# Attention and a two-layer FFN on one core: k and q of the second batch's third and fourth head pair loaded ahead of the remaining weight chunks

## The chip, the core and the metric

The kernel runs on one core of a Trainium2 chip. The metric is device time in microseconds (us) from the start to the end of the program. Three runs of the kernel before gave 899.69, 900.2 and 901.63 us; the median is 900.2 us. The core has a matrix engine (PE, with its weight loads shown as PEld), three engines for elementwise work (VectorE, shown as DVE; ScalarE, ACT; GpSimd, POOL), and SyncE (SP), which here only starts transfers (DMAs) from and to device memory. Each engine takes its instructions in a fixed order, and an instruction that waits holds up those behind it on its engine.

## The reference

```python
def _attn_ref(q, k, v):                       # 8 batches, 8 heads, 576 rows, 64 columns, float32
    q_s = softmax of q over the last axis
    k_s = softmax of k over the rows (axis 2)
    kv = np.einsum('bhsd,bhse->bhde', k_s, v)
    return np.einsum('bhsd,bhde->bhse', q_s, kv)

def _moe_ref(x, w_in, w_out):                 # x: 4608 x 512 (heads side by side)
    h = x @ w_in                              # w_in: 512 x 2048
    r = np.maximum(h, 0.0)
    return ((r * r) @ w_out)                  # w_out: 2048 x 512
```

The weights come as 64-bit floats. A product of float32 accuracy is made of three passes of a shorter format: high by high, low by high, high by low.

## The kernel before, in words

**Tiling.** The 4608 rows are taken as one block of 512 rows per batch, and a ninth block made of the 64 rows that each batch leaves over (`x_left` in device memory). Heads go in pairs, four per batch; pair `pr` of batch `b` gives 128 of the 512 columns of x. I write (1,2) for the third pair of the second batch. The FFN goes by 16 chunks `fc` of 128 hidden columns. For each chunk `ffn_h` makes h with 12 matmuls (lines 412 to 414), `activate` makes the square of the ReLU and splits it in `g_hi` and `g_lo` (lines 416 to 430), and two chunks later `ffn_out` adds 12 matmuls into four accumulators (lines 446 to 448). I call these twelve matmuls h7 or o5, by the chunk.

**Weights.** Each chunk of w_in (`raw_i`) and of w_out (`raw_o`) is a transfer of 512 KB. Such a chunk becomes two float32 halves in `split_weight` (line 156): two conversions on ACT (lines 168 and 170), two combining operations on DVE (lines 172 and 173, through the one PSUM bank `bank3`), the high part on ACT (line 180) and the low part on POOL (line 181). I call the halves wi7 or wo5. Weights are split while the first block runs, so the first 135 us hold all 32 splits, all attention work of batch 1 (the second batch), and the first of batch 2.

**Attention of batch 1.** A pair has these units: `k_max` (line 224 on DVE, a transpose on PE at line 228, line 230 on DVE), `k_spread` (line 256 on PE), `q_exp` (lines 266 on DVE, 268 on POOL, 271 on ACT), `k_exp` (line 261 on DVE, 262 on ACT), `q_norm`, `kv` (line 305 on PE), transposes of q (lines 353 and 355), and the product with kv (line 364). From batch 2 on, `k_max` finds its maximum by a chain of small DVE operations (lines 238 to 251) instead of PE.

**Buffers and loads.** k, q and v of batch 1 and later go through two buffers each (`kt0`, `kt1`, `qt0`, `qt1`, `vt0`, `vt1`); the pair two places on reuses the buffer. `load_one` starts a load, two DMAs for k or q, four for v, all from SP. In the kernel before, the load of a pair's k, q or v is called right behind the unit that reads the buffer last two pairs earlier. A pool tag `raw` has four buffers (`RAWB`), for small staging tiles: `left` (64 columns of x on their way to `x_left`) in batches 0 and 1, `tb`, `xf` and `o` later.

**Order.** Units of batch 1 stand in a table of slots (`FIRST_KV`, `EARLY_STEP`, `EARLY_AT`) and are issued with raised priority; the framework's scheduler then fixes the order of each engine's instructions by its own estimate of times. So a change in where loads are called can move instructions on every engine. PE's order in the first block is nearly fixed by `ordered`, which chains the PE instructions of batches 0 and 1.

Of the kernel before, what the change touches and what calls it, by code (L numbers as in the profile page):

```python
# [8 lines left out]
F32 = mybir.dt.float32  # L9
# [7 lines left out]
P = 128  # L17
HALF = 64
LOW = 5
# [26 lines left out]
def attention_ffn_kernel(ctx: ExitStack, tc: tile.TileContext, q, k, v, w_in, w_out, out):  # L46
# [74 lines left out]
    def load(dst, src, b, pr, n):  # L121
        s = src[b, 2 * pr : 2 * pr + 2]
        lo = s[:, :SPLIT, :].rearrange("h (p j) d -> p h j d", j=LOW)
        hi = s[:, SPLIT:, :].rearrange("h (p j) d -> p h j d", j=HIGH)
        if n < 2 or b == 0:
            e = nc.scalar if (b, pr, n) in ACT_LOADS else nc.sync
            e.dma_start(dst[:HALF], lo)
            e.dma_start(dst[HALF:, :, :HIGH, :], hi)
        else:
            for h in range(2):  # L130
                nc.sync.dma_start(dst[:HALF, h, :, :D], lo[:, h])
                nc.sync.dma_start(dst[HALF:, h, :HIGH, :D], hi[:, h])

    def tiles(b, pr):
        i = pr if b == 0 else pr % NB
        return kt[i], qt[i], (v0 if b == 0 else vt)[i]

    def load_one(b, pr, n):
        load(tiles(b, pr)[n], (k, q, v)[n], b, pr, n)

    def load_pair(b, pr):
        for n in range(3):
# [384 lines left out]
    x_hi.append(late.tile([P, NCC, NT], F32R, name="x_hi1"))  # L527
    x_lo.append(late.tile([P, NCC, NT], F32R, name="x_lo1"))

    for pr in range(NB):  # L530
        load_pair(1, pr)
    for n in range(AHEAD, NFC):
        load_more(n)
    steps = [(0, fc) for fc in order0] + [(blk, fc) for blk in range(1, B + 1) for fc in range(NFC)]
    LAG = 2
    gs, accs = {}, {}
# [2 lines left out]
    for b in range(1, B):  # L539
        for pr in range(NPAIR):  # L540
            if b == 1:
                base, offs = FIRST_KV + EARLY_STEP * pr, EARLY_AT
            else:
                base, offs = 2 * NFC * (b - 1) + 1 + STEADY_STEP * pr, STEADY_AT
            us = attention(b, pr)
            nxt = b * NPAIR + pr + NB
            if nxt < B * NPAIR:
                i = 5 if b == 1 else 4

                for i, m in ((i, 2), (i - 2, 0), (i - 3, 1)):  # L550
                    us[i] = lambda f=us[i], m=m, nxt=nxt: (f(), load_one(nxt // NPAIR, nxt % NPAIR, m))
            for u, o in zip(us, offs):
                slots.setdefault(base + o, []).append(u)
    for cc, u in enumerate(left_units()):
        slots.setdefault(2 * NFC * (B - 1) + 4 + 6 * cc, []).append(u)
# [64 lines left out]
```

## Time and profile before

| what | value |
|---|---|
| median of three runs | 900.2 us |
| the profiled execution, its own time | 900.7 us |
| its span, first to last instruction | 898.9 us |
| granted PE clock, mean over the span | 0.994 |
| PE idle in the span | 29.4 us (898.9 less 869.5 busy) |
| of that in 0 to 67 us | 13.7 us |
| of that in 67 to 90 us | 6.6 us |
| of that in 90 to 135 us | 3.4 us |
| of that from 135 to 600 us | 0 |

The table's idle times are the length of a stretch less PE's busy time in it, from the view that gives each engine's busy time by stretch. PE is the engine that sets the end: from 135 us to its last matmul it has no gap that the profile shows. What the first 135 us lose on PE, the whole run loses. In the timeline a row reads: start in us, length in us, engine, line, operation, what it writes and reads; a bracket at the end gives the engine's idle time ahead of it and what ended that.

### The profile page before, as it was taken

To read this page: it belongs to the slowest core of one execution; us is meant where nothing else is said; L and a number is where in the kernel's file an instruction comes from. 1 tells how busy PE (TensorE), PEld (TensorE's weight loads), DVE (VectorE), ACT (ScalarE), POOL (GpSimd) and SP (SyncE) were. 2 spreads that over 40 slices of the span, in tenths; PEclk is the share of its full clock that TensorE was granted. 3 is DMA by queue.
4 is the path that set the end of the run, shared out by engine and by line. 5 is a ranking of instruction groups with operands and counts; after the bars stand their busy time and mean duration, and the time that the engine had idled before them with its cause. 6 is when DMAs were issued, how large, how long until landed. Compare 5 with 4: busy or idle time off the path is not lost.

```text
span 898.9 us, 12680 instructions
## 1 busy us (share of the span) xinstructions
PE 869.5 (97%) x4368; PEld 700.6 (78%) x4368; DVE 579.6 (64%) x1177; ACT 407.7 (45%) x801; POOL 202.4 (23%) x177
## 2 busy tenths in 40 slices
PE   4997999999999999999999999999999999999997
PEld 3675677888888888888888888888888888888885
DVE  7767898877778876877688767876764242222222
ACT  3785756455345453544454544454444232222222
POOL 3676634222212220231122212221222000000000
PEclk9998999999999999999999999999999999999999
DMA  9999212422142224322333133222311030002001
GB/s 234 278 317 257 68 30 58 117 77 79 44 117 76 80 58 104 85 71 71 88 84 81 51 83 88 77 66 69 92 31 32 2 93 1 1 1 47 1 1 47
DMA packets 95743, 73.18 MB, mean 81 GB/s; under 512 B 47552, under 2 KB 85440, under 8 KB 95680
## 3 DMA queue, kind: packets, MB, share of 16 engines
q1 hardware_dynamic: 94944, 71.53, 29.5%
q10 hardware_dynamic: 736, 0.85, 0.4%
q8 instruction: 34, 0.56, 0.3%
q14 instruction: 29, 0.24, 0.1%
HBM read 54.00 MB, written 18.35 MB: 80 GB/s over the span
## 4 chain that ended last, share of the span: by engine, by line
PE 85%; DVE 1%; issue 0%; ACT 0%
PE o_ps L446 14%; PE bank L412 14%; PE o_ps L448 14%; PE o_ps L447 14%; PE bank L414 13%; PE bank L413 13%; PE bank L305 2%; PE bank L384 1%; DVE w L173 0%; DVE r L422 0%; DVE bank L172 0%; DVE m L243 0%; DVE kvn L321 0%; DVE o_last L460 0%; DVE m L246 0%
## 5 line engine op out<-in xcount | busy, mean ns | idle before, releaser
L412 PE MATMUL bank<-x_hi,wi 128*128 128x512 f32 x568 | 226.0, 398 | 2.2 <-DVE r L422 2.2
L446 PE MATMUL o_ps<-wo,g_hi 128*128 128x512 f32 x576 | 227.6, 397 | 0.0
L447 PE MATMUL o_ps<-wo,g_hi 128*128 128x512 f32 x576 | 224.9, 390 | 0.0
L448 PE MATMUL o_ps<-wo,g_lo 128*128 128x512 f32 x576 | 224.4, 391 | 0.0
L414 PE MATMUL bank<-x_hi,wi 128*128 128x512 f32 x568 | 223.4, 393 | 0.0
L413 PE MATMUL bank<-x_lo,wi 128*128 128x512 f32 x568 | 222.4, 392 | 0.0
L424 DVE TENSOR_TENSOR r<-r 128x512 f32<-128x512 f32 x128 | 110.7, 865 | 119.5 <-ACT r L418 119.2
L429 DVE TENSOR_TENSOR g_lo<-r,g_hi 128x512 fp32r<-128x512 f32 x132 | 100.7, 763 | 106.7 <-ACT g_hi L425 105.3
L425 ACT CAST g_hi<-r 128x512 fp32r<-128x512 f32 x144 | 89.2, 619 | 124.4 <-PE o_ps L447 78.2
L418 ACT ACTIVATE r<-bank 128x512 f32<-128x512 f32 x142 | 84.7, 596 | 102.5 <-PE bank L414 99.6
L412 PEld LDWEIGHTS bank<-x_hi,wi 128*128 128x128 f32 x568 | 107.1, 189 | 26.3 <-DVE r L422 3.5
L446 PEld LDWEIGHTS o_ps<-wo,g_hi 128*128 128x128 f32 x576 | 108.2, 188 | 23.5 <-issue 0.5
L448 PEld LDWEIGHTS o_ps<-wo,g_lo 128*128 128x128 f32 x576 | 108.1, 188 | 23.2
L447 PEld LDWEIGHTS o_ps<-wo,g_hi 128*128 128x128 f32 x576 | 108.2, 188 | 22.8 <-issue 0.5
L414 PEld LDWEIGHTS bank<-x_hi,wi 128*128 128x128 f32 x568 | 106.9, 188 | 24.2 <-POOL wi L181 0.4
L413 PEld LDWEIGHTS bank<-x_lo,wi 128*128 128x128 f32 x568 | 107.0, 188 | 21.9 <-issue 0.2
L395 POOL TENSOR_TENSOR x_lo<-xf,x_hi 128x256 fp32r<-128x256 f32 x48 | 39.6, 825 | 374.0 <-ACT x_hi L394 373.3
L338 POOL TENSOR_TENSOR qs<-qT,qs 64x640 fp32r<-64x640 f32 x48 | 81.8, 1705 | 60.0 <-ACT qs L337 47.1
L224 DVE TENSOR_REDUCE m<-kt 128x128 f32<-128x640 f32 x32 | 41.4, 1298 | 20.6 <-DMA kt<-in_k_dram 20.4
L337 ACT CAST qs<-qT 64x640 fp32r<-64x640 f32 x48 | 34.9, 726 | 39.6 <-DMA qT<-bounce 39.0
L271 ACT ACTIVATE qn<-qn 128x640 f32<-128x640 f32 x32 | 23.6, 739 | 54.2 <-DVE qn L268 44.8
L386 ACT COPY xf<-bank 64x320 f32<-64x320 f32 (+1 forms) x96 | 37.9, 395 | 20.6 <-PE bank L384 13.0
(118 smaller groups left out, 775.3 us busy)
## 6 DMA issues: line engine op xcount, KB each, us to landing
out_dram<-o SPq DMA_DIRECT2D x70, 128.0 KB, 2.4
raw_i<-in_moe_w_in_dram SPq DMA_DIRECT2D x16, 512.0 KB, 8.4
raw_o<-in_moe_w_out_dram SPq DMA_DIRECT2D x16, 512.0 KB, 9.6
bounce<-tb SPq DMA_DIRECT2D x24, 320.0 KB, 2.2
qT<-bounce SPq DMA_DIRECT2D x96, 80.0 KB, 2.2
kt<-in_k_dram SPq DMA_DIRECT2D x32, 160.0 KB, 3.0
qt<-in_q_dram SPq DMA_DIRECT2D x30, 160.0 KB, 3.0
vt<-in_v_dram SPq DMA_DIRECT2D x56, 80.0 KB, 2.5
```

The source lines that it names most:

```text
L224: nc.vector.tensor_reduce(m, kk.rearrange("p h j d -> p h d j"), axis=AX.X, op=ALU.max)
L338: nc.gpsimd.tensor_tensor(qs[other], qT[own], qs[own].bitcast(F32), op=ALU.subtract)
L412: nc.tensor.matmul(ps, wi[fc][:, 0, sl], xh[:, cc, :], start=(cc == 0), stop=False)
L413: nc.tensor.matmul(ps, wi[fc][:, 0, sl], xl[:, cc, :], start=False, stop=False)
L414: last.append(nc.tensor.matmul(ps, wi[fc][:, 1, sl], xh[:, cc, :], start=False, stop=(cc == NCC - 1)))
L418: nc.scalar.activation(r, ps, AF.Relu)
L424: nc.vector.tensor_tensor(r, r, r, op=ALU.mult)
L425: gh = nc.scalar.copy(g_hi, r)
L429: e.tensor_tensor(g_lo, r, g_hi.bitcast(F32), op=ALU.subtract)
L446: nc.tensor.matmul(acc[t], g_hi[:, ts], wo[fc][:, 0], start=(n == 0), stop=False)
L447: nc.tensor.matmul(acc[t], g_hi[:, ts], wo[fc][:, 1], start=False, stop=False)
L448: prev = nc.tensor.matmul(acc[t], g_lo[:, ts], wo[fc][:, 0], start=False, stop=(n == NFC - 1))
```

## The change

Batch 1's pairs (1,2) and (1,3) get k buffers of their own: two tiles `k_own2` and `k_own3` out of the four of the `raw` tag, taken at the start, with their unused corner set by POOL. After the loads of pairs (1,0) and (1,1), the program now calls the loads of k of (1,2) and (1,3). Then it issues the `q_exp` units of (1,0) and (1,1) and, behind each, the load of q of (1,2) and (1,3). Only then, held behind the last of these loads on SP, it starts the remaining weight chunks: raw_o4 to raw_o15 and raw_i8 to raw_i15. v of (1,2) and (1,3) is called where it was. `kt0` and `kt1` are no longer used by (1,2) and (1,3), so the loads of k of (2,0) and (2,1) are their next use.

```diff
-            e.dma_start(dst[HALF:, :, :HIGH, :], hi)
+            return e.dma_start(dst[HALF:, :, :HIGH, :], hi)
...
+    k_own = {}
+    for pr in range(NB, NPAIR):
+        t = w_pool.tile([P, 2, LOW, D], F32, name=f"k_own{pr}", tag="raw", bufs=RAWB)
+        nc.gpsimd.memset(t[HALF:, :, HIGH, :], -FLT_MAX)
+        k_own[1, pr] = t
+
     def tiles(b, pr):
         i = pr if b == 0 else pr % NB
-        return kt[i], qt[i], (v0 if b == 0 else vt)[i]
+        return k_own.get((b, pr), kt[i]), qt[i], (v0 if b == 0 else vt)[i]
...
+    second = [attention(1, pr) for pr in range(NPAIR)]
     for pr in range(NB):
         load_pair(1, pr)
-    for n in range(AHEAD, NFC):
-        load_more(n)
+    for pr in range(NB, NPAIR):
+        load_one(1, pr, 0)
+    for pr in range(NB):
+        with tc.high_priority(OFFSET):
+            second[pr][2]()
+        second[pr][2] = None
+        q_last = load_one(1, pr + NB, 1)
+    with tc.issue_after(q_last.ins):
+        for n in range(AHEAD, NFC):
+            load_more(n)
...
-            us = attention(b, pr)
+            us = second[pr] if b == 1 else attention(b, pr)
...
                 for i, m in ((i, 2), (i - 2, 0), (i - 3, 1)):
+                    if nxt // NPAIR == 1 and m < 2:
+                        continue
                     us[i] = lambda f=us[i], m=m, nxt=nxt: (f(), load_one(nxt // NPAIR, nxt % NPAIR, m))
             for u, o in zip(us, offs):
+                if u is None:
+                    continue
                 slots.setdefault(base + o, []).append(u)
```

The rows that follow show the order of instructions on two engines. Lines of the changed kernel are six higher from `load_one` to the end of the helpers (266 becomes 272, 224 becomes 230, 172 and 173 become 178 and 179, 422 becomes 428); the last number in a name is only a running number of the tile.

SP, from the last load of pair (1,1) on, before:

```order
L132 DMA vt1_81<-in_v_dram 64x4x64
L153 DMA raw_o4_555<-in_moe_w_out_dram 128x1024
L151 DMA raw_i8_557<-in_moe_w_in_dram 128x4x256
L153 DMA raw_o5_559<-in_moe_w_out_dram 128x1024
L151 DMA raw_i9_561<-in_moe_w_in_dram 128x4x256
```

and now:

```order
L132 DMA vt1_81<-in_v_dram 64x4x64
L127 DMA k_own2_131<-in_k_dram 64x2x320
L128 DMA k_own2_131<-in_k_dram 64x2x256
L127 DMA k_own3_133<-in_k_dram 64x2x320
L128 DMA k_own3_133<-in_k_dram 64x2x256
L127 DMA qt0_82<-in_q_dram 64x2x320
L128 DMA qt0_82<-in_q_dram 64x2x256
L379 DMA x_left_77<-left_472 128x64
L379 DMA x_left_77<-left_514 128x64
L127 DMA qt1_83<-in_q_dram 64x2x320
L128 DMA qt1_83<-in_q_dram 64x2x256
L159 DMA raw_o4_577<-in_moe_w_out_dram 128x1024
```

Eight load DMAs and two small stores now stand ahead of the first of the twenty remaining weight chunks. Before, q of (1,2) stood behind raw_o9, q of (1,3) behind raw_o10, and k of (1,2) behind raw_o14.

DVE, from the last combining of the squared ReLU of h1 on, before:

```order
L422 TENSOR_TENSOR r_618<-r_618,h_ps1_132 128x512
L280 RECIPROCAL qs_829<-qs_829 128x10
L230 TENSOR_REDUCE mc_651<-bank2_88 128x1
L172 SCALAR_TENSOR_TENSOR bank3_89<-bank3_89,raw_i4_167 128x512
L261 TENSOR_TENSOR ke_677<-kt0_78,bank2_88 128x640
```

and now:

```order
L428 TENSOR_TENSOR r_640<-r_640,h_ps1_136 128x512
L272 TENSOR_REDUCE qm_946<-qt0_82 128x10
L286 RECIPROCAL qs_833<-qs_833 128x10
L236 TENSOR_REDUCE mc_666<-bank2_88 128x1
L230 TENSOR_REDUCE m_967<-k_own2_131 128x128
L178 SCALAR_TENSOR_TENSOR bank3_89<-bank3_89,raw_i4_171 128x512
L272 TENSOR_REDUCE qm_1108<-qt1_83 128x10
L267 TENSOR_TENSOR ke_692<-kt0_78,bank2_88 128x640
```

The row maximum of q of (1,2) now stands ahead of the reduction `mc` of pair (1,0), for which PE waits at line 256 (262 now); the maxima of k of (1,2) and of q of (1,3) stand ahead of `ke` of (1,0).

DVE, between r of h7 (the first row) and the second combining step of raw_i9, before (raw_i9's is the third row from the top, r of h7 the fifth):

```order
L172 SCALAR_TENSOR_TENSOR bank3_89<-bank3_89,raw_i9_561 128x512
L224 TENSOR_REDUCE m_1148<-kt1_79 128x128
L173 SCALAR_TENSOR_TENSOR w_853<-raw_i9_561,bank3_89 128x512
L266 TENSOR_REDUCE qm_1400<-qt0_82 128x10
L422 TENSOR_TENSOR r_980<-r_980,bank0_86 128x512
```

and now:

```order
L428 TENSOR_TENSOR r_984<-r_984,bank0_86 128x512
L267 TENSOR_TENSOR ke_1013<-k_own2_131,bank2_88 128x640
L178 SCALAR_TENSOR_TENSOR bank3_89<-bank3_89,raw_o6_585 128x512
L230 TENSOR_REDUCE m_1354<-kt0_78 128x128
L179 SCALAR_TENSOR_TENSOR w_795<-raw_o6_585,bank3_89 128x512
L284 TENSOR_REDUCE qs_1180<-qn_1110 128x10
L272 TENSOR_REDUCE qm_1404<-qt0_82 128x10
L244 STREAM_TRANSPOSE mt_1356<-m_1354 128x128
L201 TENSOR_TENSOR x_lo1_542<-bank2_88,x_hi1_541 128x512
L286 RECIPROCAL qs_1180<-qs_1180 128x10
L246 TENSOR_REDUCE m1_1358<-mt_1356 128x4
L230 TENSOR_REDUCE m_1528<-kt1_79 128x128
L272 TENSOR_REDUCE qm_1584<-qt1_83 128x10
L178 SCALAR_TENSOR_TENSOR bank3_89<-bank3_89,raw_i9_583 128x512
L249 COPY m4_1360<-m1_1358 32x4 x4
L428 TENSOR_TENSOR r_1050<-r_1050,bank0_86 128x512
L179 SCALAR_TENSOR_TENSOR w_857<-raw_i9_583,bank3_89 128x512
```

Before, raw_i9 was combined ahead of r of h7; now it is combined behind r of h8 (the last row but one), and the maxima of k and q of (2,0) and (2,1), which read `kt0`, `qt0`, `kt1` and `qt1`, stand ahead of it.

More of the change, by code (lines that the diff above doesn't have):

```diff
@@ L132, in load @@
                 nc.sync.dma_start(dst[HALF:, h, :HIGH, :D], hi[:, h])
+    k_own = {}
[3 more added lines that the diff above has]
+        k_own[1, pr] = t
     def tiles(b, pr):
         i = pr if b == 0 else pr % NB
-        return kt[i], qt[i], (v0 if b == 0 else vt)[i]
+        return k_own.get((b, pr), kt[i]), qt[i], (v0 if b == 0 else vt)[i]
     def load_one(b, pr, n):
-        load(tiles(b, pr)[n], (k, q, v)[n], b, pr, n)
+        return load(tiles(b, pr)[n], (k, q, v)[n], b, pr, n)
     def load_pair(b, pr):
```

## The prediction

> **What bounds the kernel now.** I read first the busy time of each engine by stretch (columns: stretch, its length, then busy us and count for PE, PEld, DVE, ACT and POOL, granted PE clock, DMA share, GB/s), then PE's waits from 45 to 135 us (total us, times, longest).
>
> ```profile
> 67.00:90.00 23.00, 16.42 (x84) 12.54 (x83) 16.46 (x28) 12.55 (x25) 13.96 (x12) 0.85 0.96 259
> 90.00:112.00 22.00, 20.29 (x105) 15.24 (x104) 19.29 (x38) 17.50 (x35) 13.77 (x12) 1.00 0.24 66
> 112.00:135.00 23.00, 21.34 (x109) 16.18 (x108) 21.10 (x51) 13.70 (x27) 8.77 (x7) 1.00 0.12 32
> ```
>
> ```profile
> PE bank L228 <- DVE m L224: 6.3, 1, 6.3
> PE bank L412 <- DVE r L422: 2.2, 4, 1.4
> PE bank L228 <- ACT kvn L319: 1.2, 1, 1.2
> PE bank L256 <- DVE mc L230: 0.9, 1, 0.9
> ```
>
> PE carries the end, so only its gaps count. In 67 to 90 us it idles 6.6 us, 6.3 of them in one wait; the granted clock falls to 0.85 there. From 90 to 135 us DVE is busy 40.4 of 45 us: it has little room, and most of PE's 3.4 us of gaps there end on it. That second fact decides this prediction.
>
> **The wait that the change aims at.** The timeline around it, then where the load landed (last column: us from issue to landing), and the clock in the gap:
>
> ```profile
> 77.44 0.27 PE L355 MATMUL bank<-ident,qn 64*128 64x64 f32 x1
> 83.97 0.47 PE L228 MATMUL bank<-ident,m 128*128 128x128 f32 x1 [6.27 <-DVE m L224]
> 84.68 0.63 PE L413 MATMUL bank<-x_lo,wi 128*128 128x512 f32 x1
> 85.11 0.63 PE L414 MATMUL bank<-x_hi,wi 128*128 128x512 f32 x1
> 87.75 0.39 PE L413 MATMUL bank<-x_lo,wi 128*128 128x512 f32 x1
> 87.98 0.40 PE L414 MATMUL bank<-x_hi,wi 128*128 128x512 f32 x1
> ...
> 82.69 1.23 DVE L224 TENSOR_REDUCE m<-kt 128x128 f32<-128x640 f32 x1 [2.63 <-DMA kt<-in_k_dram]
> ...
> 72.49 0.61 SPq L128 DMA_DIRECT2D kt<-in_k_dram  x1
> ```
>
> ```profile
> kt<-in_k_dram SPq DMA_DIRECT2D x1, 128.0 KB, 10.2
> ```
>
> ```profile
> 80.00:81.00 1.00, 0.00 (x0) 0.00 (x0) 0.05 (x1) 1.00 (x4) 0.48 (x1) 0.50 1.05 264
> ```
>
> k of (1,2) is issued at 72.49 and lands 10.2 us later, at 82.69, behind the weight chunks; DVE starts its maximum in that instant and PE waits 6.27 us for it. The clock is at half by 80 us, and the first six matmuls of h7 then follow each other at 0.43 us instead of 0.23: another 6 x 0.2 = 1.2 us. With k loaded before the chunks both go: at most 7.5 us.
>
> **Cost one: the early loads themselves.**
>
> ```profile
> 45.00 0.61 SPq L132 DMA_DIRECT2D vt<-in_v_dram  x1
> 45.66 0.59 SPq L153 DMA_DIRECT2D raw_o<-in_moe_w_out_dram  x1
> ...
> 48.98 0.68 DVE L422 TENSOR_TENSOR r<-r,h_ps 128x512 f32<-128x512 f32 x1
> 49.70 0.23 DVE L230 TENSOR_REDUCE mc<-bank 128x1 f32<-128x128 f32 x1
> 49.99 0.49 PE L256 MATMUL bank<-ident,mc 128*128 128x128 f32 x2 [0.86 <-DVE mc L230]
> ```
>
> ```profile
> qt<-in_q_dram SPq DMA_DIRECT2D x1, 128.0 KB, 2.6
> ```
>
> SP issues a DMA every 0.65 us (45.00 to 45.66). The second half of q of (1,2) is now the sixth from 45.66, so issued at 48.9; the like load at 42.40, which the last row shows, landed in 2.6 us, so it is there at 51.5. On DVE its row maximum now stands right behind r of h1, which ends at 49.6: DVE stands still for 1.9 us. Queued behind it are the reciprocal, `mc` of (1,0), the split of raw_i4 and `ke` of (1,0). With 0.72 us for the maximum itself (the 0.80 of the row at 95.88 below, less its overlap with the next) `mc` comes at 52.4 instead of 49.70, and PE at line 256 goes on at 52.7 instead of 49.99: **2.7 us lost**. PE's gap there grows from 0.86 to 3.6 us. Whether the clock falls in 3.6 us lies between the 1.2 us gap of the waits (clock 1.00 in that stretch) and the 6.3 us gap; since it was at half 2.3 us after PE's last matmul above, I take the full 1.2 us (bounds 0 and 1.7).
>
> [...]
>
> The raw chunks start ten issues later, at 51.9. Is ACT late for it?
>
> ```profile
> 54.93 0.67 ACT L168 ACTIVATE raw_o<-raw_o 128x512 uint32<-128x512 uint8 x1
> ...
> 50.70 2.23 SPq L153 DMA_DIRECT2D raw_o<-in_moe_w_out_dram  x1
> 73.44 0.34 SPq L153 DMA_DIRECT2D raw_o<-in_moe_w_out_dram  x1
> ```
>
> ```profile
> raw_o<-in_moe_w_out_dram SPq DMA_DIRECT2D x1, 512.0 KB, 4.6
> ```
>
> ```profile
> raw_o<-in_moe_w_out_dram SPq DMA_DIRECT2D x1, 512.0 KB, 11.2
> ```
>
> ```profile
> raw_o<-in_moe_w_out_dram SPq DMA_DIRECT2D x1, 512.0 KB, 11.3
> ```
>
> The first chunk of 45.66 landed in 4.6 us, so raw_o4 now lands at 56.5. ACT reads it at 54.93 before; being 3 to 4 us late itself, it comes at 58 to 59. No wait. The two k tiles occupy half of the `raw` tag only while `left` uses it; I cost that, and two small memsets on POOL at the start, at nothing.
>
> So PE comes to line 228 of (1,2) at 77.7 + 2.7 + 1.2 = 81.6 without a wait, h7 runs at full clock (12 x 0.23) and ends at 84.5; before it ended at 88.2. **Gained there: 3.7 us**, of the 7.5.
>
> **Cost two: splits behind attention work on DVE.** Between r of h7 and the second half of raw_i9's combining the changed order has r of h8, `ke`, the split of raw_o6 and both maxima of (2,0) and (2,1). Rows for the price of each:
>
> ```profile
> 94.64 1.32 DVE L224 TENSOR_REDUCE m<-kt 128x128 f32<-128x640 f32 x1 [1.31 <-DMA kt<-in_k_dram]
> 95.88 0.80 DVE L266 TENSOR_REDUCE qm<-qt 128x10 f32<-128x640 f32 x1
> ...
> 98.25 0.68 DVE L173 SCALAR_TENSOR_TENSOR w<-raw_i,bank 128x512 uint32<-128x512 uint32 x1
> 98.85 0.68 DVE L422 TENSOR_TENSOR r<-r,bank 128x512 f32<-128x512 f32 x1
> 99.44 0.66 DVE L243 COPY m<-m 32x4 f32<-32x4 f32 x4
> ...
> 92.00 0.60 ACT L425 CAST g_hi<-r 128x512 fp32r<-128x512 f32 x1
> 93.63 0.61 ACT L180 CAST wo<-w 128x512 fp32r<-128x512 f32 x1
> 90.42 1.30 POOL L181 TENSOR_TENSOR wi<-w,wi 128x512 fp32r<-128x512 f32 x1 [0.27 <-ACT wi L180]
> ...
> 99.58 0.50 PE L412 MATMUL bank<-x_hi,wi 128*128 128x512 f32 x1 [0.49 <-DVE r L422]
> 115.85 0.51 PE L412 MATMUL bank<-x_hi,wi 128*128 128x512 f32 x1 [1.36 <-DVE r L422]
> ```
>
> From start to start: 1.24 us for a k maximum, 0.60 for a 512-wide step, 0.7 for a 640-wide one (the row maximum's 0.80 less overlap), 0.7 for the four small copies. r of h7 starts 0.8 us behind h7 (ACT's ReLU and the step between engines, an estimate), at 85.3. To the end of r of h8: six 512-wide 3.6, four 640-wide 2.9, two k maxima 2.5, copies 0.7, three tiny ones 0.5: 10.2, so 95.5. ACT stands in order: `g_hi` and two conversions (92.00 to 93.63: 1.63), the conversion of raw_o7 and the high part of wi9 (0.6 each): 98.3. PE could start h9 at 94.8 (84.5, then 36 matmuls of o5, h8 and o6 at 0.23 and 2.0 of small ones), but waits for wi9 to 98.4, and 0.7 more for POOL's 1.30 us low part, which the third pass needs. That is as good as 99.1, against 99.58 before: **3.2 of the 3.7 us are given back.**
>
> From r of h8 to r of h10, DVE has the same number of splits in both orders, and now on top the chain of small maxima of (2,1) (two groups like 99.44 and four single ones, 2.7 us), the k maximum and chain of (2,2) (1.24 + 2.7), and one half split (0.6), less the copies already counted. That is some 6.6 us on the 16.3 between those two rows before (98.85 to just ahead of 115.85), of which about 2.4 were waits of DVE that fall away. So r of h10 ends at about 95.5 + 20.5 = 116.0, and with ACT's share h11, which uses the same bank, starts near 116.9 against 115.85: **1.1 us late**, and nothing later in the two orders gives it back. Bounds for this cost: 95.5 + 16.3 (all of it hidden), which puts h11 2.7 us ahead of before's with r of h10 at 111.8 and PE's own work then ruling; and 1.9 us more, if DVE waits as in the slower rival.
>
> **Sum:** profiled execution -7.5 + 2.7 + 1.2 + 3.2 + 1.6 (0.5 ahead to 1.1 late) = 1.2 us longer: 901.9 against 900.7. The median lies 0.5 under the profiled time, so **901.4 us**. A difference of 0.2% (1.8 us) is about what a measurement here can tell from none.
>
> **Rivals.**
> *Faster.* The splits come in time, because ACT and DVE have slack that my sum of in-order steps denies them. For it: DVE idles 6.5 of 23 us in 67 to 90. Against it: that idle time lies in the wait which goes. PE would keep the 3.7 us, at best 4.9 with no clock loss: 896 to 897 us. Chance 0.23.
> *Slower.* The place is DVE's maximum of q of (2,1), which decides if it lands after about 92.5. It now stands on SP behind all twenty chunks. From 56.5 at 1.45 us a chunk (50.3 to 61.9 for eight, the issues at 45.66 and 50.70 with 4.6 and 11.2 us) raw_o15 lands at 84.1; it landed at 84.7 (73.44 + 11.3) before. SP holds an issue until the eighth one before it has landed (raw_o8 went out at 50.70, raw_o4 had landed at 50.3); the second half of q of (2,1) stands nine issues behind the one that raw_o15 holds, 5.9 us, and takes 2.6 to land: 92.6, and by the steps above DVE comes to it at 92.8, just behind. At the pace of the last four chunks before, where small loads were mixed in (about 2.1 us each), raw_o15 comes at 86.7, DVE waits 1 us for k of (2,0) and 1 to 2 for q of (2,1), and h9, h10 and h11 move by that: 903 to 904.5. Chance 0.28.
> *The change does not do what it says*: k of (1,2) arrives early but PE waits at the same place for another thing, 900 us. Chance 0.07.
>
> **How the numbers follow.** The forecast (loss and gain cancel, 899.6 to 903) has 0.42, of which 0.07 lies over 902.0. Faster: 0.23. Same: 0.35 + 0.07 = 0.42. Slower: 0.28 + 0.07 = 0.35. The range takes in most of both rivals: 896.8 to 904.6; the forecast's own is 899.6 to 903.
>
> **What would show it.** Right: no PE wait for `m` at line 228 in batch 1; a PE gap of about 3.6 us at line 256 near 50 us; a gap of 3 us or more ahead of h9 near 95 us, ended by the high part of wi9 (line 186) or r. Wrong: DVE not standing still at 49.6; h9's gap under 1 us; or DVE's waits for k and q of (2,0) and (2,1) above 2 us.

## The result, and the profile after

| | before | changed |
|---|---|---|
| median, six runs each | 901.1 us (899.69 to 901.63) | 905.6 us (904.51 to 906.41) |
| ratio to before, 95% interval | | 1.0051 (1.0038 to 1.0064) |
| profiled execution, its span | 900.7 us, 898.9 us | 904.5 us, 902.7 us |
| granted PE clock over the span | 0.994 | 0.992 |

The change makes the kernel 0.5% slower. That is clear of the 0.2% that can be told from none, and 1.0 us above the top of the stated range, 904.6. First the four largest of PE's waits in the changed kernel from 40 to 160 us (total us, times, longest), lines six higher than before:

```profile
PE bank L262 <- DVE mc L236: 4.7, 1, 4.7
PE bank L418 <- ACT wi L186: 3.2, 1, 3.2
PE bank L370 <- DVE mt L256: 1.7, 1, 1.7
PE bank L420 <- POOL wi L187: 1.0, 2, 0.6
```

The wait that the change aimed at (6.27 us, now line 234) is not among them. Three others are. Now the 90 us in one row, of the kernel before:

```profile
45.00:135.00 90.00, 79.03 (x405) 60.38 (x404) 71.89 (x144) 62.92 (x121) 52.27 (x44) 0.96 0.58 168
```

and of the changed one:

```profile
45.00:135.00 90.00, 79.33 (x392) 60.16 (x391) 69.66 (x142) 62.34 (x117) 51.29 (x43) 0.92 0.54 167
```

PE idles 90 - 79.03 = 11.0 us before and 90 - 79.33 = 10.7 us now: the gaps have moved, not shrunk. But in the same busy time PE gets fewer matmuls done, since the clock is 0.92 instead of 0.96. Over the whole span PE's busy time is 872.9 us instead of 869.5 and its idle time 29.8 instead of 29.4. That is the reading to start from: **most of the profiled 3.8 us, 3.4, is PE working slower; only 0.4 is PE waiting longer.** It is a sum over the profile and not yet a cause: the half clock itself follows gaps of PE, as the rows below show.

The first gap, DVE and PE:

```profile
48.62 0.68 DVE L428 TENSOR_TENSOR r<-r,h_ps 128x512 f32<-128x512 f32 x1
51.77 0.82 DVE L272 TENSOR_REDUCE qm<-qt 128x10 f32<-128x640 f32 x1 [2.46 <-DMA qt<-in_q_dram]
...
52.62 0.23 DVE L236 TENSOR_REDUCE mc<-bank 128x1 f32<-128x128 f32 x1
...
52.91 0.80 PE L262 MATMUL bank<-ident,mc 128*128 128x128 f32 x2 [4.72 <-DVE mc L236]
```

and the clock around it (last three columns: granted clock, DMA share, GB/s):

```profile
51.00:52.00 1.00, 0.00 (x0) 0.00 (x0) 0.23 (x1) 0.84 (x2) 0.00 (x0) 0.58 0.38 104
52.00:57.00 5.00, 4.09 (x11) 3.32 (x12) 5.00 (x9) 1.49 (x3) 2.51 (x2) 0.50 0.91 289
57.00:58.00 1.00, 1.00 (x4) 0.81 (x3) 1.00 (x3) 0.92 (x2) 0.00 (x0) 0.51 0.92 357
```

The slices inside such a stretch read 0.50 and those around it 1.00, so a slice of 1 us at 0.58 was at half for 2 x 0.42 = 0.84 us: the clock fell at 51.16 and rose at 57.98. PE was back at 52.91 and worked 5.1 us at half: 2.5 us lost. Before, by the rows

```profile
79.00:80.00 1.00, 0.00 (x0) 0.00 (x0) 0.90 (x2) 1.00 (x3) 1.00 (x2) 0.99 1.08 229
...
86.00:87.00 1.00, 1.00 (x4) 0.81 (x3) 0.36 (x1) 0.61 (x2) 0.85 (x1) 0.59 0.65 185
```

the clock fell at 79.98 and rose at 86.82, as long, but PE came back only at 83.97 and lost 1.4.

The second gap, ahead of h9:

```profile
96.65 0.69 DVE L428 TENSOR_TENSOR r<-r,bank 128x512 f32<-128x512 f32 x1
97.26 0.68 DVE L179 SCALAR_TENSOR_TENSOR w<-raw_i,bank 128x512 uint32<-128x512 uint32 x1
...
97.43 0.62 ACT L431 CAST g_hi<-r 128x512 fp32r<-128x512 f32 x1 [3.33 <-DVE r L428]
97.96 0.66 ACT L174 ACTIVATE raw_i<-raw_i 128x512 uint32<-128x512 uint8 x1
98.52 0.65 ACT L174 ACTIVATE raw_o<-raw_o 128x512 uint32<-128x512 uint8 x1
99.07 0.60 ACT L176 ACTIVATE bank<-raw_o 128x512 f32<-128x512 f32 x1
99.61 0.60 ACT L186 CAST wi<-w 128x512 fp32r<-128x512 f32 x1
...
100.27 0.79 PE L418 MATMUL bank<-x_hi,wi 128*128 128x512 f32 x1 [3.21 <-ACT wi L186]
```

```profile
98.00:99.00 1.00, 0.00 (x0) 0.00 (x0) 0.93 (x6) 1.00 (x3) 0.87 (x1) 0.97 0.30 68
99.00:105.00 6.00, 4.33 (x9) 2.98 (x10) 5.78 (x19) 3.62 (x8) 3.24 (x3) 0.50 0.35 88
105.00:106.00 1.00, 1.00 (x4) 0.66 (x2) 1.00 (x2) 0.00 (x0) 0.00 (x0) 0.61 0.00 0
```

The forecast chain is there, step for step: r of h8, the split of raw_i9 behind it on DVE, four ACT instructions, the high part of wi9, and h9 at 100.27. What the forecast did not have is the half clock from 98.94 to 105.78: h9 takes 5.98 us instead of 3.03 in the kernel before. The third gap:

```profile
108.41 1.29 POOL L187 TENSOR_TENSOR wi<-w,wi 128x512 fp32r<-128x512 f32 x1 [4.06 <-ACT wi L186]
...
108.82 2.50 DVE L249 COPY m<-m 32x4 f32<-32x4 f32 x4
...
110.01 1.30 POOL L435 TENSOR_TENSOR g_lo<-r,g_hi 128x512 fp32r<-128x512 f32 x1 [0.31 <-PE bank L359]
...
114.55 1.10 PE L370 MATMUL bank<-qT,kvn 128*128 128x512 f32 x2 [1.69 <-DVE mt L256]
```

Four small copies take 2.50 us, where the forecast had 0.7 (and 0.66 is what they take at 95.96 and 102.20). Taken one by one, two of the four are short (0.16 us each); the first takes 0.89 us and ends at 109.71, 0.01 us behind the first POOL operation shown, and the last takes 1.26 us and ends at 111.33, 0.03 us behind the second. Behind them on DVE stands `mt`, for which PE waits before o8.

### The profile page after: what moved, and what is told of

The parts are those of the page before. It is cut to its first block, busy times and chain, and to the rows that moved or that the text cites. A ratio compares the mean times of both kernels' runs of the same rounds, so it can differ in the third digit from the quotient of the medians.

```text
span 902.7 us, 12689 instructions
## 1 busy us (share of the span) xinstructions
PE 872.9 (97%) x4368; PEld 701.6 (78%) x4368; DVE 583.4 (65%) x1177; ACT 408.7 (45%) x801; POOL 202.4 (22%) x179
## 4 chain that ended last, share of the span: by engine, by line
PE 88%; DMA 4%; DVE 3%; SPq 2%; issue 2%; POOL 1%; ACT 0%; DVEq 0%; POOLq 0%; ACTq 0%
PE o_ps L452 14%; PE o_ps L454 14%; PE o_ps L453 14%; PE bank L418 14%; PE bank L420 14%; PE bank L419 14%; DMA qt<-in_q_dram 2%; PE bank L311 2%; PE bank L390 1%; DMA raw_i<-in_moe_w_in_dram 1%; SPq L127 1%; SPq L128 1%; DMA kt<-in_k_dram 0%; DVE w L179 0%; PE bank L370 0%
## 5 line engine op out<-in xcount | busy, mean ns | idle before, releaser
L230 DVE TENSOR_REDUCE m<-kt 128x128 f32<-128x640 f32 x30 | 38.9, 1296 | 14.5 <-DMA kt<-in_k_dram 14.5
```

Of the source, the lines that this page charges most:

```text
L230: nc.vector.tensor_reduce(m, kk.rearrange("p h j d -> p h d j"), axis=AX.X, op=ALU.max)
```

## The experiments

My theory before them: two wrong orders on DVE (q's maximum ahead of `mc`, batch 2's maxima ahead of raw_i9's split), each with a half clock behind it. Rivals: the early loads hurt as such; or the three engines that split weights have so much to do up to 150 us that PE waits somewhere in any case. The kernel before had medians of 900.85 to 901.02 us in the sessions that follow; a run's ratio is to the one of its session, and a difference in us is one of medians.

**One part of the change alone.** k ahead alone, with q loaded where the kernel before has it:

```diff
-    for pr in range(NB, NPAIR):
-        load_one(1, pr, 0)
-    for pr in range(NB):
-        with tc.high_priority(OFFSET):
-            second[pr][2]()
-        second[pr][2] = None
-        q_last = load_one(1, pr + NB, 1)
-    with tc.issue_after(q_last.ins):
+    k_loads = [load_one(1, pr, 0) for pr in range(NB, NPAIR)]
...
+    with ExitStack() as order:
+        order.enter_context(tc.issue_after(k_loads[-1].ins))
         for n in range(AHEAD, NFC):
             load_more(n)
...
-                    if nxt // NPAIR == 1 and m < 2:
+                    if nxt // NPAIR == 1 and m == 0:
```

> k of (1,2) and (1,3) ahead of the chunks in buffers of their own, as in the changed kernel; q of both loaded, and its maximum taken, where the kernel before has them. Theory A (the loss is made on DVE: it stands still at its queue's head for q at 50 us, PE's gap there grows from 0.9 to 4.7 us and halves the clock; later the splits stand behind the third batch's maxima): the gap at line 256 (262) is back to about 1 us with the clock at 1.00, PE reaches h7 some 5 us earlier than the changed kernel's 83.3 us, and a part of that is lost again between h7 and h13 since DVE's order there is much as in the changed kernel: 899 to 903 us. Rival B (the loads ahead of the chunks make the weight stream late, and the two buffers taken from the staging tag hold up ACT's copies): both are still so, most of the loss stays: 904 to 906 us.

901.66 us, ratio 1.001 (0.9999 to 1.0022). The gap at 49.8 is 0.68 us and the 6.27 us wait is gone, but a new one stands in its place:

```profile
61.09 0.82 DVE L272 TENSOR_REDUCE qm<-qt 128x10 f32<-128x640 f32 x1 [5.45 <-DMA qt<-in_q_dram]
...
63.85 0.48 PE L234 MATMUL bank<-ident,m 128*128 128x128 f32 x1 [4.21 <-DVE kvn L327]
```

q of (1,2) now stands behind the chunks on SP while its maximum has moved ahead of `kvn` of (1,0) on DVE. It is the first gap again, 11 us later, and with a half clock from 62.90 to 69.72. q ahead alone, k in the old buffers:

```diff
     k_own = {}
-    for pr in range(NB, NPAIR):
-        t = w_pool.tile([P, 2, LOW, D], F32, name=f"k_own{pr}", tag="raw", bufs=RAWB)
-        nc.gpsimd.memset(t[HALF:, :, HIGH, :], -FLT_MAX)
-        k_own[1, pr] = t
...
-    for pr in range(NB, NPAIR):
-        load_one(1, pr, 0)
...
-                    if nxt // NPAIR == 1 and m < 2:
+                    if nxt // NPAIR == 1 and m == 1:
```

> q of (1,2) and (1,3) ahead of the chunks and their place on DVE as in the changed kernel; k in the old buffers, no staging buffer taken. Theory A: the gap at line 256 near 50 us stays at 3 to 5 us with the clock at half behind it, some 5 us lost there; 902 to 907 us, by how the scheduler then sets k and the splits. Rival B (k's loads and the staging buffers): the loss goes, 899 to 902 us.

901.33 us, ratio 1.0003 (0.9993 to 1.0013). The time is in the range of rival B (899 to 902), but the gap that theory A expects is there: a gap of 3.00 us at line 258 (for `mc`, as in the changed kernel) and one of 5.1 us for the high part of wi11, each with a half clock of 6.82 us; the k of (1,2) comes in time here because the scheduler moved its load ahead too, behind raw_o8. So neither part alone is faster or slower than before, and neither gives the gap's 6.27 us back to the end.

**The orders on DVE.** A helper holds an instruction behind the second combining step of a named chunk's split. First only batch 2's maxima, loads as changed:

```diff
+    K_BEHIND = {(2, 0): ('o', 7), (2, 1): ('i', 12), (2, 2): ('i', 12)}
+    Q_BEHIND = {(2, 0): ('i', 9), (2, 1): ('o', 7)}
...
-            nc.vector.tensor_reduce(m, kk.rearrange("p h j d -> p h d j"), axis=AX.X, op=ALU.max)
+            with behind(K_BEHIND, b, pr):
+                nc.vector.tensor_reduce(m, kk.rearrange("p h j d -> p h d j"), axis=AX.X, op=ALU.max)
...
-            nc.vector.tensor_reduce(qm, qq, axis=AX.X, op=ALU.max)
+            with behind(Q_BEHIND, b, pr):
+                nc.vector.tensor_reduce(qm, qq, axis=AX.X, op=ALU.max)
```

> The changed kernel, with the maxima of k of (2,0), (2,1), (2,2) and of q of (2,0), (2,1) held on DVE behind the weight splits where the kernel before has them (raw_o7, raw_i12, raw_i9). Nothing else is edited, the loads are the same. Theory A: the early gap and its half clock stay, 5 us; the gap of 3.2 us ahead of h9 falls under 1 us, the clock stays at 1.00 there, and h9 ends 4 to 6 us earlier than the changed kernel's 106.2: 900 to 903 us. Rival B (late weights): wi9 is as late as before, 905 to 906 us.

903.46 us, ratio 1.0026 (1.0017 to 1.0035): 2.2 us less than the change, and 0.5 us above what I expected. h9 comes without a gap, 97.72 to 100.76 at full clock, 5.5 us earlier than in the changed kernel. The first gap stays (4.4 us). Of the 5.5 us more than half goes again, in waits of up to 1.3 us for r, wi and kvn that were not there before.

Then only the first order, batch 1's q maxima held, everything else as changed:

```diff
+    K_BEHIND = {}
+    Q_BEHIND = {(1, 2): ('i', 4), (1, 3): ('o', 2)}
```

> The changed kernel with all its loads where they are, but the row maxima of q of (1,2) and (1,3) are held on DVE behind the splits of raw_i4 and raw_o2, so that mc of (1,0) no longer stands behind a load that has not landed. If the wait at the head of DVE's queue is what costs the early stretch (my reading), PE's gap at line 262 falls from 4.72 us to about 0.9, the clock stays full and o0 with o1 takes 5.7 us instead of 7.9: 3.8 + 2.2 = 6.0 us earlier at o1, and 900 to 901 us if at least 5 of these last to the end. The rival, that the three engines which split (DVE, ACT, POOL) have more work up to 135 us than PE leaves them time for, lets PE come earlier and then wait longer ahead of h9 to h12: 903 to 905 us.

902.91 us, ratio 1.0022 (1.0013 to 1.0031): 2.7 us less than the change, between the two expectations. The early part is what I expected, to 0.4 us: the gap falls to 1.25, the clock stays full, o0 with o1 takes 5.72 us, and h7 ends at 82.41 instead of 86.35. Then PE waits for what DVE has not done:

```profile
49.85 0.49 PE L272 MATMUL bank<-ident,mc 128*128 128x128 f32 x2 [1.25 <-DVE mc L246]
...
115.95 0.80 PE L429 MATMUL bank<-x_hi,wi 128*128 128x512 f32 x1 [3.97 <-ACT wi L186]
```

h11 ends at 121.94 at half clock, against 121.67 in the changed kernel: the 3.9 us have been given back there. Both orders held:

```diff
+    K_BEHIND = {(2, 0): ('o', 7), (2, 1): ('i', 12), (2, 2): ('i', 12)}
+    Q_BEHIND = {(2, 0): ('i', 9), (2, 1): ('o', 7), (1, 2): ('i', 4), (1, 3): ('o', 2)}
```

> As the run that holds only the q maxima of (1,2) and (1,3), and the maxima of k and q of (2,0), (2,1) and k of (2,2) held behind later splits as well. If the two costs are two separate wrong orders on DVE and nothing of the early loads themselves costs time, both gaps with a half clock are gone (at line 262 and ahead of h9) and the time is 896 to 899 us, under the kernel before. If the splitting engines' whole work sets the time, waits of 1 to 3 us come up between h10 and the last split near 150 us and the time stays at 900 to 902.

898.70 us, ratio 0.9977 (0.9966 to 0.9988). This is faster than the kernel before, with all the early loads in place, so the early loads as such are not what makes the change slow. The savings were 2.7 and 2.2 us alone and are 6.9 together: repairing one order leaves the other to take the gain. In the profiled execution no half clock is left in the first 165 us. Other executions of this kernel did lose clock: the mean over the span is 1.000 in the profiled one and 0.993 to 0.998 in the other eight, of which a half clock behind PE's last matmul may explain 0.001 to 0.002: in the profiles of the kernel before and of the changed one it lasts 3.1 and 1.6 us there, 0.0017 and 0.0009 of the span. One gap of it is worth a look:

```profile
99.40 0.33 PE L244 MATMUL bank<-ident,m 128*128 128x128 f32 x1 [3.21 <-ACT kvn L336]
```

```profile
96.00:99.00 3.00, 0.18 (x1) 0.04 (x1) 2.88 (x15) 1.34 (x3) 0.11 (x1) 1.00 0.32 73
...
100.00:103.00 3.00, 3.00 (x18) 2.49 (x16) 3.00 (x6) 1.22 (x3) 1.45 (x2) 1.00 0.01 3
```

The same 3.21 us as ahead of h9 in the changed kernel, and the clock does not fall.

k ahead alone (the edit of the first run), with batch 2's maxima held:

```diff
+    K_BEHIND = {(2, 0): ('o', 7), (2, 1): ('i', 12), (2, 2): ('i', 12)}
+    Q_BEHIND = {(2, 0): ('i', 9), (2, 1): ('o', 7)}
```

> Both edits together: k alone ahead of the chunks, and the third batch's maxima held behind the splits. Theory A: neither gap is there, the wait of 6.3 us of the kernel before is gone: 895 to 899 us, faster than both kernels. Rival B: 903 us or more. Rival C (DVE and ACT simply have too much to do before 135 us, so what is saved at one place comes back at another): 899 to 902 us.

899.80 us, ratio 0.9985 (0.9974 to 0.9995): slightly faster than the kernel before, but in the range of rival C (899 to 902) and above that of theory A. And this with q's maximum of (1,2) held too:

```diff
-    Q_BEHIND = {(2, 0): ('i', 9), (2, 1): ('o', 7)}
+    Q_BEHIND = {(2, 0): ('i', 9), (2, 1): ('o', 7), (1, 2): ('i', 5)}
```

> k of (1,2) and (1,3) alone ahead, q where the kernel before has it, the maxima of batch 2 late, and q's maximum of (1,2) held on DVE behind the split of raw_i5, so that kvn of (1,0) no longer stands behind it. In the run without this hold (899.8 us) PE waited 3.15 us at line 244 for kvn and then ran o2 at half clock (5.47 us instead of 2.73). If that wait costs what it seems to, up to 5 us are to be had there, of which later waits for splits take some: 896 to 898.5. If the splitting engines' whole work sets the time, it stays within 1 us of 899.8.

900.85 us, ratio 1.0002 (0.9993 to 1.0010), a miss for the first theory. The wait of 3.15 us at line 244 near 62 us is gone and no half clock is left there in the profiled execution, yet nothing is gained: the waits for r, wo, wi and kvn from 40 to 165 us add up to 9.7 us, the longest 1.3. This is what the rival says, that the splitting work sets the time, and for this kernel nothing speaks against it.

**How full DVE is.** The changed kernel with less for DVE:

```diff
+                m5 = attn_pool.tile([P, 4, 1], F32, name="m5", bufs=1)
+                if b == 2:
+                    nc.vector.tensor_copy(m5[:, :, 0], m1)
-                for g in range(4):
+                for g in range(0 if b == 2 else 4):
                     nc.vector.tensor_copy(m4[:, g], m1[g * BLK : (g + 1) * BLK])
-                m5 = attn_pool.tile([P, 4, 1], F32, name="m5", bufs=1)
-                for g in range(4):
+                for g in range(0 if b == 2 else 4):
                     nc.vector.tensor_reduce(
...
```

> The changed kernel with less work for DVE: in batch 2 the eight small operations that gather a pair's maxima from four groups of partitions are left out and one copy of the ungathered maxima stands in their place, so the output of batch 2 is not the reference's. Nothing else moves up to r of h9 in DVE's order. That takes about 1.2 us off DVE per pair, 0.6 of it ahead of the second combining step of raw_i9 and some 3 us up to h11. If DVE's in-order work is what holds h9 to h12 back (my reading), h9 starts 0.5 us or more earlier, the wait of 1.69 us at line 370 ahead of o8 and the late start of h11 go, and the time falls from 905.6 to 901 to 903.5. The rival, that the splits are late by ACT, POOL or the loads, leaves 905 to 906.

902.37 us, ratio 1.0016 (1.0008 to 1.0025), 3.3 us less than the change. h9 starts 1.1 us earlier, the wait ahead of o8 is gone. This run also leaves out the small copies that stood still in the third gap, so its gain cannot be told from theirs (see the next runs); and its profiled execution, 900.35 us, was the fastest of eleven. And the kernel before with more for DVE:

```diff
+            if (b, pr) in ((2, 0), (2, 1)):
+                for _ in range(2):
+                    nc.vector.tensor_reduce(m, kk.rearrange("p h j d -> p h d j"), axis=AX.X, op=ALU.max)
```

> The kernel before with more work for DVE: the maxima of k of (2,0) and (2,1) are taken three times instead of once, 2.5 us more at either, at about 96 and about 110 us. If DVE has no room between 90 and 135 us, most of these 5 us shows up as PE's waits for splits or r: 903 to 906 with a longer wait ahead of h10 or h11. If the splits have slack there, 901 to 902.

906.96 us, ratio 1.0074 (1.0061 to 1.0087), above the expected range. The 5 us added cost 6.1. So what DVE does between 90 and 135 us is on the path in the kernel before; in the changed kernel the run with less points the same way. The extra 1.1 may go with something that the next runs take up: the small copies of this run took 1.45, 1.79 and 1.79 us (0.66, 1.11 and 0.71 before).

**The small copies.** The same numbers, computed by a reduction over one element, every engine's order as in the changed kernel:

```diff
-                    nc.vector.tensor_copy(m4[:, g], m1[g * BLK : (g + 1) * BLK])
+                    nc.vector.tensor_reduce(
+                        m4[:, g], m1[g * BLK : (g + 1) * BLK].rearrange("p (c o) -> p c o", o=1), axis=AX.X, op=ALU.max
+                    )
```

> The changed kernel with the four small copies of a pair's maximum (32x4) made by VectorE's reduction over one element instead of its copy; the numbers computed are the same and the order of all engines is kept. In the changed kernel's trace the four at 108.82 us took 2.50 instead of 0.66 us, two of them until POOL's operation of that moment ended. If the copy stands still for POOL and the reduction does not, the four take about 0.7 us there, PE's wait of 1.69 us at line 370 ahead of o8 falls to under 0.3, and the time falls by 1 to 2 us, to 903.5 to 905. If the small operations are long for another reason, they stay at 2.5 and the time at 905.6.

902.46 us, ratio 1.0021 (1.0012 to 1.0030): 3.2 us less than the change, from four tiny operations a pair.

```profile
107.62 1.28 POOL L187 TENSOR_TENSOR wi<-w,wi 128x512 fp32r<-128x512 f32 x1 [4.08 <-ACT wi L186]
108.86 1.31 POOL L437 TENSOR_TENSOR g_lo<-r,g_hi 128x512 fp32r<-128x512 f32 x1
...
108.04 0.61 DVE L249 TENSOR_REDUCE m<-m 32x4 f32<-32x4 f32 x4
...
112.24 1.10 PE L372 MATMUL bank<-qT,kvn 128*128 128x512 f32 x2 [0.59 <-DVE mt L258]
```

The four run in 0.61 us beside POOL's work, and PE's wait falls from 1.69 to 0.59, not to under 0.3. Part of the 3.2 us of the two medians is other: in this profile the two half clocks lasted 3.4 us instead of 6.8. Executions of the two kernels at the same mean clock, 0.990 to 0.992, took 903.1 us (four, mean) and 905.3 (five), so some 2 us are left for the copies. The larger copy of each pair (128x128, line 256 in the changed kernel) stands still as well: 0.82 and 0.76 us at 98.68 and 103.66, to 0.08 and 0.07 us behind the end of a POOL operation (99.42 and 104.35), where it takes 0.22 at 114.32, behind one that ended at 114.29. This run leaves it as it is, at 0.82 us twice.

**PE's gaps and the clock.** Two tries to take the half clock away alone. One moves PE's step at line 262 a slot later, in all four pairs of batch 1, so that o0 fills the gap:

```diff
-FIRST_KV, EARLY_STEP, EARLY_AT = 7, 5, (-4, -3, -5, -3, -3, 0, 1, 2, 3, 4)
+FIRST_KV, EARLY_STEP, EARLY_AT = 7, 5, (-4, -2, -5, -2, -3, 0, 1, 2, 3, 4)
```

> The changed kernel, with PE's matmuls of line 262 and the product after it one slot later, so that PE has the twelve matmuls of o0 (2.9 us) to do while DVE waits for q of (1,2). If PE's idle time and the clock that it loses are the cost, the gap of 4.72 us shrinks to about 1.9 and no matmul near 55 us runs at half clock: 2.9 + 2.2 = 5.1 us earlier at o1. DVE's own stand still stays. If that stand still is the cost, since it puts every split 2.5 us later, h9 still waits for wi9 and starts within 1 us of 100.3, and the time is 904 to 906; if PE's gap is the cost, 900 to 902.

911.63 us, ratio 1.0116 (1.0102 to 1.0129). It failed as a test. The gap is 0.44 us and o0 runs at full clock, but the moved steps find their PSUM bank in use:

```profile
PE bank L262 <- DVE x_lo L201: 12.1, 3, 5.3
```

The other puts idle matmuls into both gaps, with DVE's and ACT's order unchanged:

```diff
+            if (b, pr) == (1, 0):
+                idle = ps_o.tile([P, DM], F32, name="idle", tag="o")
+                for _ in range(1):
+                    last.append(nc.tensor.matmul(idle[:, :256], gs[1][0][:, :P], x_hi[0][:, 0, :256], start=True, stop=True))
...
+        if (blk, fc) == (0, 9):
+            for _ in range(2):
+                last.append(nc.tensor.matmul(ps[:, :512], gs[max(k for k in gs if steps[k][1] != 9)][0][:, :P], x_hi[0][:, 0, :512], start=True, stop=True))
```

> The changed kernel with three idle matmuls on PE in its two gaps, written to banks that are not read before they are overwritten: one of 256 columns ahead of line 262, which waits for g_hi of h1 (cast on ACT at 49.65 to 50.26 us), and two of 512 columns ahead of h9, which wait for g_hi of h8 (98.05). They split the gap of 4.72 us into about 2.1 and 2.5 and that of 3.21 into about 1.0 and 1.7. DVE and ACT keep their order and nothing else is touched, so mc and wi9 come when they came. If the half clock comes from gaps of PE of over some 3 us, o0 with o1 takes 5.7 us instead of 7.89 and h9 3.0 instead of 5.98, 2.2 and 2.9 us: 905.6 falls to 901 to 903, less what later waits on DVE take back. If one short matmul does not keep the clock, or the clock falls for another reason, o0 with o1 stays near 7.9.

904.72 us, ratio 1.0045 (1.0032 to 1.0057), within 1 us of the change. The gaps were split as meant (1.37 and 1.69 us; 1.06 and 1.45), and the clock fell all the same, at 51.20 for 6.8 us and at 102.40 for 3.4.

```profile
50.16 0.38 PE L265 MATMUL idle<-x_hi,g_hi 128*128 128x256 f32 x1 [1.37 <-ACT g_hi L435]
52.23 0.79 PE L266 MATMUL bank<-ident,mc 128*128 128x128 f32 x2 [1.69 <-DVE mc L236]
```

The two matmuls of the second row take 0.79 us, where they took 0.80 in the changed kernel and 0.49 at full clock. So these short matmuls did not keep the clock up, and no run changes the clock alone.

The executions on record say something about its price all the same, since executions of one kernel have the same orders and their clocks differ. Take as lost by the clock the span times one less its mean granted clock. Over 132 executions of the sixteen kernels other than the kernel before (one of 4900 us left out), each counted from its own kernel's mean, 1 us more lost goes with 0.28 us more time (standard error 0.06). Some of it is lost behind PE's last matmul, where it costs nothing, so the price inside the run is somewhat higher than that, but by this estimate far from one for one, as it would be if later waits take much of it back. Last, the idle matmuls with the reductions in place of the copies as well (both edits as shown):

> Both edits. If the half clock in two places and the copies that wait for POOL are what the prediction did not count, the sum of its own steps is what is left: 900 to 902 us, near the forecast of 901.4. If the later splits on DVE set the time in any case, it stays above 903.

902.86 us, ratio 1.0021 (1.0012 to 1.0031), between the two expectations. Beside the run with the idle matmuls alone the copies are worth 1.9 us, beside the changed kernel 3.2.

**A version that beats both.** All loads as changed, both orders held, batch 2's maxima later still, in two steps:

```diff
-    K_BEHIND = {(2, 0): ('o', 7), (2, 1): ('i', 12), (2, 2): ('i', 12)}
-    Q_BEHIND = {(2, 0): ('i', 9), (2, 1): ('o', 7), (1, 2): ('i', 4), (1, 3): ('o', 2)}
+    K_BEHIND = {(2, 0): ('i', 10), (2, 1): ('i', 12), (2, 2): ('o', 12)}
+    Q_BEHIND = {(1, 2): ('i', 4), (1, 3): ('o', 2), (2, 0): ('i', 9), (2, 1): ('i', 10)}
```

> As the run with both sets of maxima held (898.7 us), with the k maxima of (2,0), (2,1) and (2,2) behind the splits of raw_i10, raw_i12 and raw_o12 and the q maximum of (2,1) behind that of raw_i10. In the run before, DVE stood still 1.35 us for q of (2,1) with the sum of kv of (1,2) queued behind it, and PE waited 3.2 us for kvn. If that is the same head-of-queue wait once more, the 3.2 us at line 244 shrinks to under 1 and the time is 896 to 898. If DVE's work up to the last split sets the time, it stays within 1 us of 898.7.

896.62 us, ratio 0.9945 (0.9932 to 0.9958); one of the six executions took 4900.54 us, and without it the median is 896.32. The time is as expected, though the wait for kvn shrinks only to 1.5 us. The second step:

```diff
-    K_BEHIND = {(2, 0): ('i', 10), (2, 1): ('i', 12), (2, 2): ('o', 12)}
-    Q_BEHIND = {(1, 2): ('i', 4), (1, 3): ('o', 2), (2, 0): ('i', 9), (2, 1): ('i', 10)}
+    K_BEHIND = {(2, 0): ('o', 8), (2, 1): ('o', 11), (2, 2): ('o', 12)}
+    Q_BEHIND = {(1, 2): ('i', 4), (1, 3): ('o', 2), (2, 0): ('i', 9), (2, 1): ('o', 8)}
```

> The same with the maxima still later: k of (2,0) and q of (2,1) behind the split of raw_o8, k of (2,1) behind raw_o11, k of (2,2) behind raw_o12, so that the splits of raw_o7, raw_i10 and raw_o8 stand ahead of all attention work of batch 2. If the order on DVE is the cost, 896 to 898 and no PE wait of over 1 us between 95 and 135 us; what could come late instead are the transposes of q of (2,0) at line 381, by 1 to 3 us, and then the time stays at 898 to 900.

896.05 us (894.52 to 897.93), ratio 0.9944 (0.9932 to 0.9956): 4.8 us faster than the kernel before, and not told apart from the first step.

```profile
45.00:135.00 90.00, 85.59 (x452) 64.49 (x450) 73.88 (x141) 68.53 (x129) 55.16 (x47) 1.00 0.58 178
```

PE idles 4.4 us of the 90 instead of 11, the clock does not fall in them in this execution, and every small copy of these 90 us took 0.15 to 0.16 us. A wait of 2.4 us for r near 137 is what is left of DVE's backlog.

## Why the prediction was wrong

The signs that were named for a right prediction all came: no PE wait for `m`, the gap near 50 us, and the gap ahead of h9 that the high part of wi9 ends. What failed are sizes: the clock behind the two gaps, which the sum has at 1.2 and at nothing, and the small copies.

**The wait goes, and DVE stands still at 49.6 instead.** Right. PE resumed at 52.91 against 52.7 forecast; DVE waited 2.46 us, not 1.9. PE's gap was 4.72 us, not 3.6, mostly because PE had come to it 0.9 us earlier.

**The clock after the first gap, taken as 1.2 us with 1.7 as the upper bound.** This step failed. PE lost 2.5 us there. I took the price of the 6.27 us gap for a shorter one, as if a shorter gap could only cost less. The upper bound of 1.7 us had no row of the kernel before behind it. The rows show a half clock of 6.8 us in both kernels. PE lost half of what was left of it when PE came back: half of 2.85 us before, of 5.1 now.

**h7 at 84.5.** It ended at 86.2, read as the forecast reads ends, by the start of the next matmul (86.35 with the modelled end that the experiments above use). Of the 1.7 us, 1.3 are the clock, 0.2 the later `mc`, and the rest is a wait of 0.63 us for POOL's low part of a w_in half at 69 us, less small waits that went.

**The gap ahead of h9.** Mechanism and size right: 3.6 us and 0.7 for POOL's part forecast, 3.21 and 0.41 measured, at times 1.9 us later as h7 was. But the step "that is as good as 99.1" had no clock cost, a term left at nothing without a reason, and this is the larger failure: h9 took 5.98 us, 2.9 more than before, of which 0.4 are the wait for POOL and 2.5 the clock. I had a bound for the clock at the first gap and none for a gap of the same length that I had forecast myself 45 us later.

**The splits up to h11, 1.1 us late.** 2.7 us late. The sum of DVE's work was of the right kind, as the run with more of it shows; the term "0.7 for the four small copies" was mis-sized, with 2.50 us measured. Before, 0.66 stood in the row that I read; the copies at 122.04 us, which took 1.11 there, I did not look at.

**"Nothing later in the two orders gives it back", and nothing after 135 us.** Both wrong in part. h13 was 1.7 us late, 1.0 less than h11. From 170 us on PE is 3.8 us late, so another 2.1 us went between them. The gaps that the profile shows there are 1.1 us, all between 145 and 158 us, where the kernel before has none: 0.63 us in a wait for `kvs`, which DVE makes, and 0.34 in waits for POOL's low parts of w_out halves. What the rest is stays open.

**The rivals.** The slower one is not what happened, although its time was the nearest: DVE waited for no load of (2,0) or (2,1) in this stretch. The faster one named the right price, 896 to 897 us, for an order on DVE that this change does not have; with that order it is 896.05. That the splits' work sets the time in any case, which I had not listed, fits the run with q late (900.85) but not the best one.

What the runs do not settle is how the 4.2 us between forecast and result divide. The clock (1.3 more than forecast at the first gap, 2.5 at h9) and the copies (1.9 to 3.2 by medians) are more than that together. They lie on one chain, and a later wait takes back part of each; by the estimate above, it takes back more than half of the clock's.

## What to carry to other kernels

When a load is moved ahead, look at the order of the engine that reads it first. Here a row maximum that waited 2.46 us for its data held up all behind it on DVE, and PE idled 4.72 us: the 128 KB saved from the queue's end came back as a wait of its successor. When two orders on the same engine are wrong, repair both before judging the change: alone they gave 2.7 and 2.2 us, together 6.9. And look for what follows a gap of PE, not only at its length: a half clock that lasted on behind it made PE lose 2.5 us here at a gap of 4.72 us and 1.4 at one of 6.27, though by the estimate above only part of that reached the end.

## What was new of the hardware

**The half clock came in two lengths.** Read from slices of 1 us as above, the 22 stretches at half clock between 40 and 165 us, in all profiles of this case, lasted 3.40 to 3.42 us (8) or 6.82 to 6.84 (14), nothing else. In the seven profiles with more than one they start a whole number of the short lengths apart, to within 0.01 of one: in the changed kernel 98.94 - 51.16 = 47.78 us, 14 x 3.413. Gaps of one size were followed by one or not: 3.21 us at 97.06 was, and at 96.18 in another kernel (both orders held) was not. Two gaps of 1.98 us show best that it went by where they fell, the same wait in two kernels, one with a half clock behind it (k ahead with batch 2's maxima held) and one without (both orders held). The windows are counted in whole lengths from a change of the clock in the same profile, in the second kernel from one outside 40 to 165 us that no row here shows:

```profile
122.97:126.38 3.41, 1.44 (x7) 0.85 (x5) 3.28 (x10) 2.13 (x4) 0.93 (x1) 1.00 0.00 0
126.39:129.80 3.41, 3.41 (x6) 2.09 (x7) 3.28 (x10) 2.74 (x5) 1.60 (x2) 0.50 0.00 0
```

```profile
121.83:125.24 3.41, 2.62 (x12) 1.81 (x10) 3.19 (x11) 1.00 (x2) 0.14 (x1) 1.00 0.00 0
125.24:128.65 3.41, 2.22 (x7) 1.34 (x8) 3.37 (x7) 3.27 (x7) 2.56 (x2) 1.00 0.00 0
```

The first gap lies in one window, in which PE was busy for 1.44 of 3.41 us, and the clock is at half in the next. The second is shared by two windows, in which PE was busy for 2.62 and 2.22 us, and the clock stays. So it does behind a gap of 2.56 us in the run with less for DVE (96.61 to 99.17 us): counted from its own fall at 50.58, two windows share it, with PE busy for 1.66 and 1.99 us.

The windows ahead of a fall were not all idle throughout: in the one before 98.94 PE worked until 97.06, 1.5 of 3.4 us. In the windows ahead of all 22 falls PE was busy for 46% at most; of those between 40 and 165 us in which it was busy for 49% or more none was followed by a fall, and one with 42% was not either (from 90.58 us, in the run with PE's step at line 262 a slot later). An idle matmul of 0.38 us in the first gap changed neither the fall (at 51.20 instead of 51.16) nor its length (6.8 us); with two of 0.73 us in all at h9 the clock fell at 102.40 instead of 98.94 and stayed at half for 3.4 us instead of 6.8. Why it falls no run shows.

**A small copy on VectorE stood still beside POOL's work.** The twelve small copies (32x4) of the changed kernel from 85 to 135 us took 157 ns in the median and 1257 at most, and the two long ones, 0.89 and 1.26 us, end within 0.03 us of the end of a POOL operation. Reductions of the same shape did not wait: at the same place, with POOL at work from 107.62 to 108.90 us, four of them took 0.61 us, where the four copies took 2.50. What makes the copy wait no run shows.
